# Two attentions in one kernel: sliced token loads, a later value half, a moved gate and another planner rule

## The chip, the cores and the metric

The kernel runs on one core of a Trainium2 chip. The metric is the device time of one execution in microseconds. The core has a matrix engine (TensorE, PE), whose weight loads the profile shows apart (PEld), a vector engine (VectorE, DVE), a scalar engine that makes the exponentials (ScalarE, ACT), a general engine (GpSimd, POOL), and a queue that issues most transfers (SyncE, SP). Every engine works through its own list of instructions in order.

## The reference

Two attention layers over 2048 tokens with 640 features and 32 heads of 20 stand side by side; their outputs are joined.

- A, "infini": the tokens come in four segments of 512. Within a segment, softmax attention with a causal mask; besides, a memory of all earlier segments is read with phi(q), and both are mixed by a gate g of its own for each head.
- B, "sliding block": causal attention in which a token sees the last 256 tokens.

```python
phi = lambda t: where(t > 0, t + 1.0, exp(t))
g = sigmoid(beta)
for s in range(4):                         # A, segment s
    a_dot = softmax(qs @ ks.T * scale + mask) @ vs
    a_mem = (phi(qs) @ M) / (phi(qs) @ z + 1e-6)
    o = g * a_mem + (1 - g) * a_dot
    M += phi(ks).T @ vs;  z += phi(ks).sum()
A = concat(o) @ A_wo
p = softmax(where((0 <= i - j) & (i - j < 256), q @ k.T * scale, -1e9))   # B
B = (p @ v) @ B_wo
out = concat([A, B])
```

## The kernel before, in words

The work is cut into eight chunks of 512 tokens, which alternate: A0, B0, A1, B1, A2, B2, A3, B3 (numbered 0 to 7). For each chunk there are these stages.

- Token load (`load_x`): the chunk's transposed tokens, five tiles of 128 features, into one of two buffers `xT`; 640 KB for A, 720 KB for B. Only chunk 0 is loaded as five transfers, the others as one each.
- Projections (`qk_job`, `v_job`, matmuls in `wide`, L795): q and k as five pieces of 128 columns, each five matmuls of 512 columns and a copy from PSUM by VectorE (L449); v in two halves of 16 heads, each four token tiles of five matmuls of 320 columns, with a copy (L624 for A, L629 for B). For A, v is scaled by 1-g as it is copied.
- Regroup (`regroup`): the heads are held in eight groups of four. Groups 0 to 4 lie in the projected pieces as they come. The parts of groups 5 to 7 are spread over all five pieces; once piece 4 is copied, four stores bring them to memory (L404) and four loads bring them back (L412).
- Scores (`score_batch`, L687): 20 visits a chunk, 160 in all, in a fixed order. Each fills two PSUM tiles `sc` of 1024 columns; ScalarE makes an exponential of each (L703) into a tile `pt` from a ring of 12. Masks are laid on `pt` by GpSimd (L738) or, for the window's ends, by VectorE (L720).
- Value products (`av`, L752, and `av_tile`, L773): `pt` times values, with the sum of weights as a 21st column. VectorE transposes the result (`turn`, L808) into a tile `tt`, takes the reciprocal (`norm`, L834), and GpSimd multiplies it into the output `o` (L844).
- For A: phi of k and q (`phi`; exponential L469, VectorE L484 and L490). phi(k) goes to memory (L543), comes back transposed (L538), and `dm_job` adds to the memory `mz` (L592); GpSimd writes it, with a block mask `bm` and a gate factor `ez`, into the bf16 operand `MZ4` (L598, L601). `mem` multiplies phi(q) with it; `norm` adds an epsilon to the denominator (L828), and the product `u` is added to `o` (L857).
- Output (`final`, `final_job`): `o` goes to memory (L875), comes back transposed (L894) as `oT`, and each of its four token tiles is multiplied with `wo`, 2 x 5 matmuls of 320 columns. As long as scores remain, this goes through the two banks `m` and VectorE copies (L950); after the last scores it goes through `sc`, and ScalarE or VectorE copies (L933, L937), whichever the planner has as free. An output tile `ot` (ring of 4) is stored by L1015. The last token tile of chunk 7 goes another way (`last_job`).

No instruction order is written out by hand. While the program is built, a planner (`Flow`) keeps a clock for each engine and for the transfers, with a cost for each operation (`on_pe`, `on_act`, `on_dve`, `on_pool`, `on_dma`). The loop in `body` takes, at each step, the next score visit if its operands are due, then the first waiting value product, then the next step of the first job whose need is met. A value product is put off, while TensorE is in full-width mode, if a score visit is due within 1500 ns. Queued loads are issued when they are due or when the transfers' backlog is under 2500 ns (`load_time`). Rings of buffers (`piece`, `ring`) are counted in the same clock. So a changed cost or limit can move instructions anywhere.

Of the kernel before, what the change touches and what calls it, by code (L numbers as in the profile page):

```python
# [8 lines left out]
ACT = mybir.ActivationFunctionType  # L9
# [14 lines left out]
GW = G * DH  # L24
EPS = 1e-6
NPT = 12
NTT = 5
QPOOL = 750.0
GAP = 48
NM = 20  # L30
MEM2 = [(1, 6), (0, 5), (1, 7), (0, 6)]
R2 = 120
NE = 3
NOT = 4
NSC = 3

# [21 lines left out]
class Flow:  # L58
# [3 lines left out]
    def __init__(self):  # L62
        self.pe = self.act = self.dve = self.pool = 0.0
        self.mode = None
        self.sp = self.fabric = 0.0
        self.landed = []
        self.bank_free = [0.0, 0.0]
        self.open = False
        self.left = 0
        self.later = []  # L70
        self.idle_dve = []
        self.idle_low = []
        self.blocked = []
        self.loads = []
        self.seq = 0
        self.load = {}
        self.slow = {}

    def full_rate(self, t):

# [5 lines left out]
                    self.slow[m] = had < (0.355 if self.slow.get(m - 1, True) else 0.31)  # L86
        return not self.slow[k]

    def on_pe(self, mode, ns, cols, ready=0.0):
        if mode != self.mode:  # L90
            self.pe += 97.0
            self.mode = mode
        self.pe = max(self.pe, ready)
        k = int(self.pe // STRETCH)
        self.load[k] = self.load.get(k, 0.0) + cols / 2.4
        if not self.full_rate(self.pe):
            ns += cols / 2.4
        self.pe += ns
        return self.pe + 215.0
# [40 lines left out]
    def load_time(self):  # L140

        if not self.loads:
            return None
        t = max(self.sp - 100.0, self.fabric - 2500.0)
        gate, _, due = self.loads[0]
        if gate:
            if gate() is None:
                return None
            return min(max(t, gate() - 400.0), gate() + due)
        return min(t, due)  # L150
# [34 lines left out]
class _K:  # L185
# [67 lines left out]
    def load_x(self, n):  # L253

        kind, c = self.chunks[n]
        x0 = SH if kind == "A" else 0
        src = (self.xin[kind][:, c * L:(c + 1) * L] if kind == "A" else
               self.xin[kind][c]).rearrange("(kt p) s -> p kt s", p=P)
        t = self.xs[n] = self.big.tile([P, self.KT, XC], BF16, name="xT", bufs=2)

        def main():
            if n == 0:
                for kt in range(self.KT):
                    self.nc.sync.dma_start(out=t[:, kt, x0:XC], in_=src[:, kt, :])
                    self.mark(self.f.on_dma(1, 450.0, 0.0, 400.0), n, "x", kt)
                self.mark(self.done[(n, "x", self.KT - 1)], n, "x")
                return
            self.nc.sync.dma_start(out=t[:, :, x0:XC], in_=src)
            tl = self.f.on_dma(1, 2220.0 if kind == "A" else 2440.0, 0.0, 530.0)
            self.mark(tl, n, "x")  # L270
            self.mark(tl, n, "xt")
        self.loads.insert(0, (None, main, max(12000.0, self.f.pe + 6000.0)))

    def consts_mem(self):

        nc, cp = self.nc, self.cp

        def select(t, pattern, base, mul):
            nc.gpsimd.affine_select(out=t, in_=t, pattern=pattern, compare_op=ALU.is_ge,
                                    fill=0.0, base=base, channel_multiplier=mul)
        own = cp.tile([P, 4], F32, name="own")
        nc.gpsimd.memset(own[:], 1.0)
        select(own[:], [[-HD, 4]], 0, 1)
        select(own[:], [[HD, 4]], DH - 1, -1)
        self.bm = bm = cp.tile([P, self.KT + 4, 4], F32, name="bm")
        self.ez = cp.tile([P, self.KT + 4, 4], F32, name="ez")
        nc.gpsimd.tensor_copy(out=bm[:, 0:self.KT, :],  # L290
                              in_=own[:].unsqueeze(1).to_broadcast([P, self.KT, 4]))
        sel = bm[:, self.KT:, :]
        nc.gpsimd.memset(sel, 1.0)
        select(sel, [[-2 * DH, 4], [-DH, 4]], 2 * DH, 1)
        select(sel, [[2 * DH, 4], [DH, 4]], -DH - 1, -1)
        self.eps = cp.tile([P, G], F32, name="eps")

    def consts_e(self):

        nc, e = self.nc, self.e32  # L300
        for x0, x1, g in [(0, self.KT, 0)] + [(self.KT + x, self.KT + x + 1, g)
                                              for x, (_, g) in enumerate(MEM2)]:
            n = x1 - x0
            h = e[:, 4 * g:4 * g + 4 * n].rearrange("p (x j) -> p x j", j=4)
            nc.gpsimd.tensor_tensor(out=self.ez[:, x0:x1, :], in0=self.bm[:, x0:x1, :], in1=h,
                                    op=ALU.mult)
        for j in range(4):
            rows = slice(HD * j, HD * j + HD)
            nc.gpsimd.tensor_single_scalar(
                out=self.eps[rows, :], in_=e[rows, :].rearrange(  # L310
                    "p (g j) -> p g j", j=4)[:, :, j], scalar=EPS, op=ALU.mult)

    def consts_mz(self):
        nc, cp = self.nc, self.cp
# [30 lines left out]
    def load_beta(self, beta):  # L345
# [3 lines left out]
        e = self.cp.tile([P, H], F32, name="e32")  # L349
        self.nc.scalar.activation(out=e[:], in_=b[:], func=ACT.Exp, scale=-1.0)  # L350
        self.e32 = e

    def consts_beta(self):
        nc, cp, e = self.nc, self.cp, self.e32
# [105 lines left out]
    def phi(self, in_, t, m, use):  # L460
# [13 lines left out]
        def one(in_, e, es, m, ta):  # L474
            box = []

            def s1():
                r = out(m)
                if r is None:
                    r, slot = self.piece("r", 2, 1)  # L480
                    box.append(slot)
                    r = r[:]
                box.append(r)
# [68 lines left out]
    def dm_job(self, seg, pkT, v):  # L552
# [12 lines left out]
        for some in (own, [(lambda kt, h=h: spare[:, kt, R2 * h:R2 * h + R2], R2,  # L565
# [23 lines left out]
            else:  # L589
# [5 lines left out]
        t = f.dve + 138.0  # L595
        yield self.known(2 * seg, "avs")
        blk, mz = self.blk, self.mz
        nc.gpsimd.tensor_tensor(out=blk[:, :, :, DH], in0=mz[:, :, :, DH], in1=self.ez[:],  # L598
                                op=ALU.mult)
        f.on_pool(150.0, t)  # L600
        nc.gpsimd.tensor_tensor(out=blk[:, :, :, 0:DH], in0=mz[:, :, :, 0:DH],  # L601
                                in1=self.bm[:].unsqueeze(3)
                                .to_broadcast([P, KT + 4, 4, DH]), op=ALU.mult)
        self.mark(f.on_pool(1700.0), "dm", seg)

# [71 lines left out]
    def score_batch(self, n, ent, kof, q, masks):  # L677
# [13 lines left out]
                                 skip_group_check=ref[0] in "lu")  # L691
            cols += nq
        if ent[0][1][0] in "lu":
            t = f.on_pe("row64", 40.0 * len(ent), cols / 2)
        else:
            t = f.on_pe("row", cols / 2.4 + 10.0 * len(ent), cols)
        lo = min(e[4] for e in ent)
        hi = max(e[4] + e[3] for e in ent)
        pts = []
# [43 lines left out]
    def av(self, parts, g, vof):  # L743
# [4 lines left out]
        for n_, (ref, q0, nq, c0, pts) in enumerate(parts):  # L748
# [6 lines left out]
                                 start=(n_ == 0), stop=(n_ == len(parts) - 1),  # L755
                                 tile_position=(0, HD * j), skip_group_check=True)
            cols += nq
        f.on_pe("col", cols / 2.4 + 6.0 * len(parts), cols)
        return O, bi

    def av_tile(self, parts, qt, g0, vof):
# [3 lines left out]
        for gi in range(4):  # L765
            own = sorted((p[:5] for p in parts[g0 + gi] if p[1] // P == qt),
                         key=lambda e: -e[2])
            for n_, (ref, q0, nq, c0, pts) in enumerate(own):
                v = vof(ref)
                o0 = gi * P + q0 - qt * P  # L770
                for j in range(4):
# [3 lines left out]
                                     rhs=pts[j // 2][:, j % 2, c0:c0 + nq],  # L775
                                     start=(n_ == 0), stop=(n_ == len(own) - 1),
                                     tile_position=(0, HD * j), skip_group_check=True)
                f.on_pe("col", nq / 2.4 + 6.0, nq)
        return O, bi

    def mem(self, g):
# [31 lines left out]
    def norm(self, turned, dst, add_to, last, g=None):  # L813
# [11 lines left out]

        def s1():
            if add_to:
                nc.vector.tensor_tensor(out=rr[:], in0=tv[:, :, DH],  # L828
                                        in1=self.eps[:, g:g + 1].to_broadcast([P, NB]),
                                        op=ALU.add)  # L830
                f.on_dve(100.0, t0)
                nc.vector.reciprocal(out=rr[:], in_=rr[:])
            else:
# [4 lines left out]
        def s2(t1):  # L838
            to, uslot = dst, None
            if add_to:  # L840
                while self.ring("u", 3) is None:
                    self.adds[0]()
                to, uslot = self.piece("u", 3, 1, BF16, (P, NB, DH))
            nc.gpsimd.tensor_tensor(out=to[:] if add_to else to, in0=a, in1=b, op=ALU.mult)  # L844
            t2 = f.on_pool(QPOOL, max(t1, uslot["free"]) if add_to else t1)
            self.done_with(slot, t2)
# [250 lines left out]
    def seed(self, n):  # L1097
# [13 lines left out]
        else:  # L1111
# [2 lines left out]
                  ("k", self.wA["k"], self.kA, self.phi_k(n, self.scr["pk"][c], self.pkT)  # L1114
                   if c < NSEG - 1 else None)]
            v = [self.wv_A, self.vA, True, [tx, avs, self.known("dm", c - 1)]]
        for half, pieces in enumerate(((0, 1, 2), (3, 4))):
            for what, w, dst, phi in qk:
                need = [tx, gate] + ([self.known("wB" + what, 0)] if n == 1 else [])
                add(self.qk_job(n, what, pieces, w, dst, need, self.scr[what + kind][c], phi))  # L1120
            if n == 1:
                v[3] = v[3] + [self.known("wBv", half)]
            add(self.v_job(n, half, *v))

    def body(self, xA, A_wq, A_wk, A_wv, A_wo, A_beta, xB, B_wqkv, B_wo, out2d):
# [45 lines left out]
        self.consts_mem()  # L1171
        f.on_pool(8000.0)
        f.on_dve(3000.0)
        self.load_x(1)
        self.loads[:] = self.loads[1:] + self.loads[:1]
        self.wB = {}
        pieces = lambda w: w.rearrange("p (m k c) -> p m k c", m=KT, k=KT)
        self.wB["k"] = self.load_qk("wBk", pieces(B_wqkv[1]), 0, KT, None, 17000.0)
# [27 lines left out]
        for m in range(KT):  # L1206
            first("k", m, self.kA, pk0)
            first("q", m, self.qA, None)
            if m in (1, 3):
                half = m // 2  # L1210
                add(self.job(self.v_job(0, half, self.wv_A, self.vA, True,
                                        [self.known(0, "x"), self.known("wv_A", half)])))

        bs = self.batches(chunks)
        free_after = {}
# [15 lines left out]
        while True:  # L1231
# [3 lines left out]
            if i < len(bs):  # L1235
                n, ent, ms, complete = bs[i]
                kind, c = chunks[n]
                if self.ring("pt", NPT) is not None:
# [2 lines left out]
                        for w in "kq":  # L1241
                            need.append(self.done.get((n, w, e[0])))
                    if None not in need:
                        t = max(need)
                        if t <= f.pe:
                            if n != started:
                                started = n
# [18 lines left out]
            if pend:  # L1266
# [10 lines left out]
                    need = [self.done.get(("dm", c - 1)),  # L1277
                            self.done.get((n, "pq", g) if g < KT else (n, "pq2"))]
                if None not in need and not (f.open and 0 < f.left <= 3):
                    t = max(need + [min(f.bank_free)])  # L1280
                    wait = (f.mode == "full" and soon is not None and len(pend) < 3
                            and soon < f.pe + 1500.0 and self.more(f.pe))
                    if t <= f.pe and not wait:
                        pend.pop(0)
                        self.one_group(n, kind, c, g, what, parts, left, o_t, groups_done,
# [196 lines left out]
```

## Time and profile before

| | us |
|---|---|
| median of 3 runs | 351.1 (349.35 to 351.61) |
| the profiled execution | 350.9, span 349.2 |
| busy: TensorE / ScalarE / GpSimd / VectorE | 327.0 / 312.0 / 280.3 / 269.1 |
| first exponential of scores starts | 10.44 |
| last exponential of scores ends | 334.14 |
| mean granted TensorE clock | 0.99 of full speed |

Times in the profile count from the start of the span. A line of the timeline merges instructions of one kind in a row; L-numbers are lines of the kernel before. A busy TensorE includes the latency of its pipeline, so matmuls that follow each other are better read from start to start.

### The profile page before, as it was taken

The page shows a single profiled execution, that of the slowest core. Times are in us where ns is not written, and L with a number is a line of the kernel's source. Part 1 is how long each engine was busy: PE and PEld are TensorE (multiplying, and loading weights), DVE is VectorE, ACT ScalarE, POOL GpSimd, SP SyncE. Part 2 cuts the span into 40 slices and gives each one's busy share as a digit, 9 for nine tenths or more (in the row PEclk, how much of TensorE's full clock was granted, in tenths as well). Part 3 has the DMA queues.
Part 4 walks back from the last instruction along what each step waited for, and adds up shares of the span by engine and source line. Part 5 has one row for each costly group of instructions (what it writes and reads, how often), then busy time and mean ns, then how long its engine had stood idle before and what let it go on. Part 6 is the DMA issues. An engine that isn't in the chain of part 4 may idle for free.

```text
span 349.2 us, 13489 instructions
## 1 busy us (share of the span) xinstructions
PE 327.0 (94%) x5593; PEld 167.4 (48%) x5593; DVE 269.1 (77%) x564; ACT 312.0 (89%) x345; POOL 280.3 (80%) x584
## 2 busy tenths in 40 slices
PE   6999999998999999999979999989999999999895
PEld 1433445454544345455633435545553435666573
DVE  5667568988967999998836898997867998976552
ACT  1898399999899999999969999999999999999731
POOL 2399379997788989995857989999978889799640
PEclk9999999999999999999989999999999999999899
DMA  7944736565695433057683316112543028466642
GB/s 227 344 185 84 191 67 186 135 137 128 156 210 115 81 82 116 2 116 134 176 206 77 78 30 166 27 35 46 100 113 78 2 40 206 117 154 134 156 131 98
DMA packets 70186, 42.49 MB, mean 122 GB/s; under 512 B 47437, under 2 KB 68077, under 8 KB 70125
## 3 DMA queue, kind: packets, MB, share of 16 engines
q1 hardware_dynamic: 68829, 40.65, 47.3%
q10 hardware_dynamic: 1296, 0.99, 0.9%
q8 instruction: 43, 0.70, 0.9%
q14 instruction: 18, 0.15, 0.1%
HBM read 17.62 MB, written 16.96 MB: 99 GB/s over the span
## 4 chain that ended last, share of the span: by engine, by line
PE 32%; DVE 14%; ACT 13%; POOL 8%; issue 4%; DMA 2%; ACTq 0%; SPq 0%; DVEq 0%
PE m L795 17%; ACT pt L703 13%; PE sc L687 7%; POOL pt L738 5%; PE m L752 4%; DVE tt L808 3%; PE sc L795 2%; DVE pt L720 2%; POOL o L844 1%; DMA out_dram<-ot 1%; DVE ot L950 1%; PE m L773 1%; DVE kA L449 1%; DVE vU L657 1%; DVE pq L490 1%
## 5 line engine op out<-in xcount | busy, mean ns | idle before, releaser
L703 ACT ACTIVATE pt<-sc 128x1024 bf16<-128x1024 f32 (+1 forms) x320 | 295.8, 1099 | 20.8 <-PE sc L687 18.3
L738 POOL TENSOR_SCALAR_AFFINE_SELECT pt<-pt 128x256 bf16<-128x256 bf16 x448 | 200.2, 472 | 49.6 <-ACT pt L703 42.1
L808 DVE STREAM_TRANSPOSE tt<-m 128x512 f32<-128x512 f32 x88 | 60.6, 707 | 18.6 <-PE m L752 12.3
L844 POOL TENSOR_TENSOR o<-tt,rr 128x320 bf16<-128x320 f32 x64 | 48.4, 758 | 6.2 <-DVE rr L834 6.0
L795 PEld LDWEIGHTS <-xT 128*128 128x128 bf16 x350 | 31.3, 97 | 22.1 <-issue 10.3
L687 PE MATMUL sc<-qB,kB 20*64 20x64 bf16 (+2 forms) x1728 | 39.8, 218 | 2.1 <-issue 1.4
L687 PE MATMUL sc<-qA,kA 20*128 20x128 bf16 (+3 forms) x512 | 37.4, 302 | 1.1 <-ACT pt L703 0.5
L950 DVE CAST ot<-m 128x320 bf16<-128x320 f32 x52 | 24.9, 484 | 14.3 <-PE m L795 11.4
L687 PEld LDWEIGHTS <-kB 20*64 20x64 bf16 (+1 forms) x1728 | 22.3, 99 | 27.3 <-issue 25.5
L795 PEld LDWEIGHTS <-oT 128*128 128x128 bf16 x280 | 25.1, 99 | 15.5 <-issue 4.8
L795 PE MATMUL m<-xT,wk_A 128*128 128x512 bf16 x100 | 26.3, 380 | 3.1 <-DMA wk_A<-in_A_wk_dram 1.5
L795 PE MATMUL m<-wv_A,xT 128*128 128x320 bf16 x160 | 27.0, 300 | 1.8 <-DVE vA L624 0.8
L795 PE MATMUL m<-xT,wq_A 128*128 128x512 bf16 x100 | 26.5, 381 | 0.3 <-DVE mz L592 0.3
L795 PE MATMUL m<-xT,wBq 128*128 128x512 bf16 x100 | 25.8, 380 | 0.8 <-DVE tt L808 0.5
L795 PE MATMUL m<-xT,wBk 128*128 128x512 bf16 x100 | 26.4, 389 | 0.1
L795 PE MATMUL m<-wBv,xT 128*128 128x320 bf16 x160 | 26.0, 300 | 0.3 <-DVE tt L808 0.2
L687 PEld LDWEIGHTS <-kA 20*128 20x128 bf16 x512 | 11.3, 92 | 30.0 <-issue 29.0
L720 DVE TENSOR_TENSOR pt<-pt,ends 128x1024 bf16<-128x1024 bf16 x32 | 24.9, 790 | 0.0
L795 PE MATMUL m<-wo_A,oT 128*128 128x320 bf16 x130 | 22.8, 307 | 0.7 <-DVE vA L624 0.5
L752 PE MATMUL m<-pt,vA 128*32 128x256 bf16 (+3 forms) x512 | 23.3, 302 | 0.2 <-DVE qA L449 0.2
L795 PE MATMUL m<-wo_B,oT 128*128 128x320 bf16 x120 | 21.0, 306 | 0.5 <-DVE ot L950 0.5
L449 DVE CAST qB<-m 128x512 bf16<-128x512 f32 x20 | 13.7, 687 | 7.5 <-PE m L795 7.5
(104 smaller groups left out, 410.7 us busy)
## 6 DMA issues: line engine op xcount, KB each, us to landing
scr_o<-o SPq DMA_DIRECT2D x28, 160.0 KB
out_dram<-ot SPq DMA_DIRECT2D x28, 160.0 KB
xT<-in_B_x_dram SPq DMA_DIRECT2D x4, 720.0 KB
scr_pk<-e SPq DMA_DIRECT2D x15, 128.0 KB
xT<-in_A_x_dram SPq DMA_DIRECT2D x3, 640.0 KB
scr_kA<-kA SPq DMA_DIRECT2D x16, 60.0 KB
scr_qA<-qA SPq DMA_DIRECT2D x16, 60.0 KB
kA<-scr_kA SPq DMA_DIRECT2D x16, 60.0 KB
```

The source lines that it names most:

```text
L449: nc.vector.tensor_copy(out=dst[:, m, at:at + L], in_=ps[:, :])
L490: nc.vector.tensor_tensor(out=r if len(box) == 1 else e, in0=r, in1=e, op=ALU.min)
L657: self.nc.vector.tensor_copy(out=out, in_=in_)
L687: nc.tensor.matmul(ps[j // 2][h0:h1, j % 2, c0:c0 + nq], lhsT=k[rows, g, kc + h0:kc + h1], rhs=q[rows, g, q0:q0 + nq], start=True, stop=Tr ...
L703: nc.scalar.activation(out=pt[:, :, lo:hi], in_=ps[i][:, :, lo:hi], func=ACT.Exp, scale=self.scale)
L720: nc.vector.tensor_tensor(out=blk, in0=blk, in1=self.ends[:].unsqueeze(1).to_broadcast([P, 1024 // SH, SH]), op=ALU.mult)
L738: nc.gpsimd.affine_select(out=blk, in_=blk, pattern=pat, compare_op=ALU.is_ge, fill=self.zero, base=base, channel_multiplier=mul)
L752: nc.tensor.matmul(O[HD * j:HD * j + HD, q0:q0 + nq], lhsT=v[:, VS * h:VS * h + HD], rhs=pts[j // 2][:, j % 2, c0:c0 + nq], start=(n_ == 0 ...
L795: self.nc.tensor.matmul(ps[:, 0:n], lhsT=lhsT, rhs=rhs, start=start, stop=stop)
L808: self.nc.vector.transpose(out=tt[:], in_=O[:, :])
L844: nc.gpsimd.tensor_tensor(out=to[:] if add_to else to, in0=a, in1=b, op=ALU.mult)
L950: nc.vector.tensor_copy(out=ot[:, 320 * hf:320 * hf + 320], in_=ps[:, 0:320])
```

## The change

- Token loads: every chunk's load is five transfers, queued one by one with due times 1500 ns apart. The allowed backlog of the transfers falls from 2500 to 800 ns (`BACK`).
- Chunk 0's second value half is no longer put behind piece 3; it is queued by `late_v` once the first k and q pieces of chunk 1 are queued (`AT = 0`). Chunk 1's q and k jobs come piece by piece, k and q in turn.
- Gate: `ez` is now made of exp(beta) (`g32`) and multiplies the memory's numerators (MZ4's columns 0 to 19), the plain mask its denominators; the epsilon becomes a constant, the tile `eps` and its operations go.
- Planner: `room` holds back value products and half-width score visits while more than 160 matmul instructions would have been issued within 3000 ns; a value product is put off if a visit is due within 2200 ns.
- Rings: `tt` and `rr` 5 to 4 (`NTT`), `e` 3 to 2 (`NE`), `u` 3 to 2, `r` 2 to 1.
- The copies out of PSUM keep their engines and rules.

```diff
+AT = 0
+FETCH = 160
+FETCH_NS = 3000
+BACK = 800.0
-NTT = 5
+NTT = 4
-NE = 3
+NE = 2
...
+    def room(self, n):
+        while self.issued and self.issued[0][0] <= self.pe - FETCH_NS:
+            self.issued.pop(0)
+        have = n + sum(k for _, k in self.issued)
+        t = self.pe
+        for t0, k in self.issued:
+            if have <= FETCH:
+                break
+            have -= k
+            t = t0 + FETCH_NS
+        return t
...
-        t = max(self.sp - 100.0, self.fabric - 2500.0)
+        t = max(self.sp - 100.0, self.fabric - BACK)
...
+        def part(kt):
+            self.nc.sync.dma_start(out=t[:, kt, x0:XC], in_=src[:, kt, :])
...
-            self.nc.sync.dma_start(out=t[:, :, x0:XC], in_=src)
...
+        self.loads[0:0] = [(None, lambda kt=kt: part(kt), due + 1500.0 * kt)
+                           for kt in range(self.KT)]
...
-        nc.gpsimd.tensor_tensor(out=blk[:, :, :, DH], in0=mz[:, :, :, DH], in1=self.ez[:],
+        nc.gpsimd.tensor_tensor(out=blk[:, :, :, DH], in0=mz[:, :, :, DH], in1=self.bm[:],
...
-                                in1=self.bm[:].unsqueeze(3)
+                                in1=self.ez[:].unsqueeze(3)
...
-                nc.vector.tensor_tensor(out=rr[:], in0=tv[:, :, DH],
-                                        in1=self.eps[:, g:g + 1].to_broadcast([P, NB]),
-                                        op=ALU.add)
+                nc.vector.tensor_single_scalar(out=rr[:], in_=tv[:, :, DH], scalar=EPS,
+                                               op=ALU.add)
...
+            for some in ([(m,) for m in pieces] if first else [pieces]):
+                for what, w, dst, phi in qk:
...
+                if first and some[0] == AT:
+                    add(self.late_v())
...
-            if m in (1, 3):
-                half = m // 2
-                add(self.job(self.v_job(0, half, ...)))
+            if m == 1:
+                add(self.job(v(0)))
+        self.late_v = lambda: v(1)
...
-                        t = max(need)
+                        t = max(need + [f.room(4 * len(ent)) if ent[0][1][0] in "lu" else 0.0])
...
-                    t = max(need + [min(f.bank_free)])
+                    t = max(need + [min(f.bank_free), f.room(
+                        4 * len(ps_)) if what != "mem" else 0.0])
                     wait = (f.mode == "full" and soon is not None and len(pend) < 3
-                            and soon < f.pe + 1500.0 and self.more(f.pe))
+                            and soon < f.pe + 2200.0 and self.more(f.pe))
```

## The prediction

> **What bounds the kernel now.** I read the page's first part, then ScalarE's timeline from end to end, then the other engines' timelines where ScalarE is idle, then the tail. Columns of a timeline line: start, length, engine, source line, operation, count, and in brackets the idle time before it with what ended it.
>
> ```profile
> PE 327.0 (94%) x5593; PEld 167.4 (48%) x5593; DVE 269.1 (77%) x564; ACT 312.0 (89%) x345; POOL 280.3 (80%) x584
> ```
>
> ScalarE makes 320 exponentials (two for each of 160 score visits). They run back to back over long stretches: 72 of them take 66.56 us, 0.924 each, so a visit costs ScalarE 1.85 us. First start 10.44, last end 334.14. TensorE's 94% also counts pipeline latency, but it is a close second: between visits it usually has 1.4 to 2.0 us of work. So the span is 10.4 of filling, then ScalarE's work plus the moments when it gets no scores, then a tail of 15.1 without exponentials. Those moments are short but for two:
>
> ```profile
> 32.34 3.77 ACT L703 ACTIVATE pt<-sc 128x1024 bf16<-128x1024 f32 x4
> 41.58 1.94 ACT L703 ACTIVATE pt<-sc 128x1024 bf16<-128x1024 f32 x2 [5.46 <-PE sc L687]
> ...
> 180.98 1.94 ACT L703 ACTIVATE pt<-sc 128x1024 bf16<-128x1024 f32 x2 [3.04 <-PE sc L687]
> ```
>
> The first is at visit 12 (counted from 0). Visit 12 needs head groups of q and k that go to memory and back after the fifth projection piece:
>
> ```profile
> 29.18 0.69 DVE L449 CAST kA<-m 128x512 bf16<-128x512 f32 x1 [0.46 <-PE m L795]
> 30.70 0.69 DVE L449 CAST qA<-m 128x512 bf16<-128x512 f32 x1 [0.82 <-PE m L795]
> ```
>
> ```profile
> 29.90 1.67 SPq L404 DMA_DIRECT2D scr_kA<-kA  x4
> 31.67 1.96 SPq L404 DMA_DIRECT2D scr_qA<-qA  x4
> 33.73 0.41 SPq L268 DMA_DIRECT2D xT<-in_A_x_dram  x1
> 34.25 1.92 SPq L412 DMA_DIRECT2D kA<-scr_kA  x4
> 36.73 2.67 SPq L412 DMA_DIRECT2D qA<-scr_qA  x4
> ```
>
> Last load issued at 39.40, exponentials 2.2 us later. The second is at visit 81: a copy of an output tile waits until the tile buffer's previous store has landed, and TensorE's PSUM bank with it.
>
> ```profile
> 170.79 0.40 SPq L268 DMA_DIRECT2D xT<-in_A_x_dram  x1
> 172.88 0.96 SPq L1015 DMA_DIRECT2D out_dram<-ot  x2
> ```
>
> ```profile
> 177.81 0.89 DVE L950 CAST ot<-m 128x320 bf16<-128x320 f32 x2 [2.65 <-DMA out_dram<-ot]
> ```
>
> The store was issued behind a whole token load of 640 KB. In the tail TensorE is the bound: 320-column output products, (2.74-0.30)/18 = 0.136 us each.
>
> ```profile
> 342.81 2.74 PE L795 MATMUL sc<-wo_B,xT 128*128 128x320 bf16 x19
> ```
>
> ```profile
> 345.59 0.69 ACT L933 CAST ot<-sc 128x640 bf16<-128x640 f32 x1 [2.15 <-PE sc L795]
> ```
>
> **The change, part by part.** The kernel's own planner lays the order out, so all edits move instructions. Against before, TensorE's order is the same through visit 5; it differs in visits 6 to 56; from 57 to 153 it has the same kinds in the same places; it differs again in the tail.
>
> *Later second values of chunk 0.* The 20 products of the second value half (20 x 0.136 = 2.7 us) leave the place ahead of k and q piece 4 and come after the first B pieces. Working in after's order: value products end 22.6 as before; k piece 4 (5 x 0.216 = 1.1) ends 23.7, its copy (0.69) about 24.6; q piece 4, with a visit between, ends 25.1. Its copy stands on VectorE behind a memset (1.20), a reciprocal and three small operations, so it ends about 27.6. On SP the four stores of k go at 24.8, the token keys of pieces 2 and 3 stand among the other stores, the stores of q end about 29.4, k's loads take 1.9 after the landing of its stores, and q's go from about 31.4 (stores landed, as 2 us after issue now) to 33.2. With the same 2.2 us behind the last issue, visit 12 has its scores for ScalarE at 35.4 to 36.4. ScalarE itself is ready at 35.3 to 35.9 (23.18 at visit 6, six visits, one e of 0.63, at most 0.6 of waiting at visit 9 for a PSUM bank). I take 36.3 in place of 41.58: -5.2. TensorE agrees: from visit 11 to 12 it had 21 x 0.216 + 7 x 0.136 + 0.66 + 0.33 = 6.5 us of work, now 4 x 0.216 + 0.66 + 0.33 = 1.9. Bounds: -6.3 (visit 12 at ScalarE's own pace) and -2 (q's loads 3 us later). If the lead is there, next late are the value products of groups 4 to 7, which the score-tile ring of 12 (six visits) covers.
>
> *The second block, visits 12 to 40.* What TensorE no longer does early it does here: summed with the trace's median time from start to start of each kind of product, it has 52.7 us here, 49.5 before. Before, the stretch took 57.4 us (scores of visit 12 at 40.7, of visit 41 at 98.1), with 1.7 us of small ScalarE waits in it.
>
> ```profile
> 57.00:74.00 17.00, 16.66 (x349) 8.84 (x346) 15.68 (x30) 16.98 (x21) 16.86 (x34) 1.00 0.63 164
> 74.00:98.10 24.10, 22.14 (x476) 12.07 (x475) 20.40 (x44) 22.93 (x29) 19.61 (x46) 1.00 0.60 154
> ```
>
> (Busy PE, PEld, DVE, ACT, POOL.) ScalarE, TensorE and GpSimd are all near full in the first row. The phi exponentials (1.06 and 0.65) also move from visits 25 to 35 to visits 29 to 40, where after puts its heavier TensorE stretches (2.1 to 2.5 us), so they hide each other. I take -0.3; bounds -1.7 and +3.2.
>
> *Token loads in slices.* Seven loads become 35 DMAs: 28 more issues of about 0.42 us, 12 us of SP's queue, and each DMA also waits for the one eight before it. Where they stand matters: the chunk-2 load now goes behind q's and k's loads instead of ahead (part of the -5.2), and at visit 80 two output stores go ahead of four of the five slices. The tile buffers there are now four different ones, and the first reused was stored several microseconds earlier with 128 KB instead of 640 KB in front of it. So the 2.65 us wait goes; the stretch has 2.6 us of TensorE work for 1.85 of ScalarE, so not all 3.04 comes back: -2.4 (bounds -3.0 and -1.0). At the start the slices stand before the B weights; those are first used at 25.1 and 27.6, and the DMA engines run dry at about 22.3 now (share 0.09 from 22 to 24), so 3 us of delay are covered; past that each microsecond costs one.
>
> [...] In this trace, slices of 128 KB with others in flight moved 317 to 337 GB/s from 6 to 10 us. [...]
>
> *Gate in the numerators.* Four GpSimd operations (0.9 us) go, one exponential of 128x32 (0.23) comes where ScalarE waits for 4.65 us, 24 additions of 0.365 become scalar additions (nearest rows 0.17 and 0.37). VectorE is 77% busy and behind others: 0, at best -0.5.
>
> *Smaller rings.* Transposed tiles 5 to 4, e 3 to 2, u 3 to 2, r 2 to 1. Counting in the trace from each transpose back to the GpSimd product four tiles earlier, the closest are 0.61, 0.62, 0.63 and 0.80 us (303.6, 287.4, 209.9, 227.0 us); for u two back, 2.78. So 0 while GpSimd is no later than now; without that cover, see below.
>
> *Tail.* After the last visit TensorE now has 90 of the 320-column products, before 65: three output tiles fewer are done in the middle. Five come before the last value products instead of 20, so 25 x 0.136 = +3.4, all after the last token tile (53 instead of 19). Bounds +2.7 (better clock) and +4.5 (the transposed load of chunk 6 now issues behind a store and another load and lands about a microsecond ahead of need).
>
> Sum: -5.2 - 0.3 - 2.4 + 3.4 = -4.5 on a span of 349.2, so 344.7. The profiled execution took 350.9, 1.7 more than its span, and the median of the runs is 351.1. Forecast 346.5.
>
> **The rivals.**
>
> *The second block takes it back.* If TensorE or GpSimd sets the pace from 36 to 98 us, the 3.2 us come on top instead of -0.3: 350.0. For it: GpSimd busy 16.86 of 17.00. Against: ScalarE's own need there (29 visits x 1.85, less 0.43 for each of eight short ones, plus 5.1 of phi: 55.4) is still more than TensorE's 52.7. 17%.
>
> *Everything helps.* Visit 12 at -6.3, second block -1.7, visit 81 -3.0, tail +3.0: 349.2 - 8.0 + 1.7 = 342.9. 13%.
>
> *It doesn't do what it says.* SP is in order; if the token-key stores between the k and q stores wait for VectorE, q's loads go as late as now and -5.2 becomes about -0.7: 351.0. 7%.
>
> *Slower: the ring of four.* A transpose that finds its buffer still in use blocks VectorE, with it the PSUM bank and TensorE. The blocker is a product standing on GpSimd behind up to four selects, 4 x 0.445 = 1.8 us. It decides once GpSimd runs 0.7 us later than now, at 4 places; at 2.6 us later at 7 (next margins 2.46, 2.59, 2.59). 4 to 7 x 1.8 = 7 to 13, so 353.7 to 359; I take 356. For it: GpSimd is saturated in the B chunks. Against: the margins are positive everywhere now. 18%.
>
> **How the numbers follow.** The forecast holds 45%, between 345 and 349. One per cent, 3.5 us, is about what a measurement of this kernel can tell from no change; the border is 347.6. Faster: 13 + three quarters of 45 = 47%; same: the rest of it, 17 and 7, 35%; slower 18%. The range reaches from the best case to the lower part of the slow one: 342.5 to 354.5.
>
> **What would show it.** Right: visit 12's exponentials at 35.5 to 37; no VectorE wait on an output store near visit 80 and under 1 us of ScalarE wait at visit 81; visit 40 five to six microseconds earlier; 18 to 19 us from the last exponential to the end. Wrong: transposes that wait for GpSimd products, visit 12 after 38, visit 40 less than 3 us ahead, or a tail that waits for a transposed load.

## The result and the profile after

The changed kernel took 345.7 us in the median of 4 runs (344.84 to 347.2), the kernel before 351.2: ratio 0.9859, 95% interval 0.9811 to 0.9908. Measured again with the experiments it took 346.4 beside 350.2, ratio 0.9926 (0.9893 to 0.9960). Ratios leave out disturbed runs, so they need not be those of the medians. So the gain was 1.4% in the first measurement and 0.7% in the second. The profiled execution took 345.8, span 344.1, against 350.9 and 349.2.

The page's first part; ScalarE is now busy for 91% of the span:

```profile
PE 319.8 (93%) x5555; PEld 165.6 (48%) x5593; DVE 266.8 (78%) x560; ACT 312.7 (91%) x347; POOL 278.5 (81%) x580
```

ScalarE's timeline of the changed kernel, the lines around the two waits that the prediction was about, and then the waits of about 1 us:

```profile
30.34 36.18 ACT L727 ACTIVATE pt<-sc 128x1024 bf16<-128x1024 f32 x40 [1.05 <-PE sc L711]
...
159.28 59.03 ACT L727 ACTIVATE pt<-sc 128x1024 bf16<-128x1024 f32 x64
...
243.46 57.19 ACT L727 ACTIVATE pt<-sc 128x1024 bf16<-128x1024 f32 x62 [1.08 <-PE sc L711]
301.51 7.55 ACT L727 ACTIVATE pt<-sc 128x1024 bf16<-128x1024 f32 x8 [0.86 <-POOL pt L762]
...
315.79 9.62 ACT L727 ACTIVATE pt<-sc 128x1024 bf16<-128x1024 f32 x10 [0.96 <-PE sc L711]
```

The 40 exponentials that run on from 30.34 hold visit 12, which starts at 35.99; the 5.46 us are gone. The 64 from 159.28 hold visit 81; the 3.04 us are gone. Idle time of ScalarE between the first and the last exponential fell from 16.2 to 7.7 us. Three waits of about 1 us are new; the prediction had none of them.

The granted clock of TensorE differs too. This row of the page gives it for 40 slices of the span (9 is full), for the kernel before and then for the changed one:

```profile
PEclk9999999999999999999989999999999999999899
PEclk9999999999999999999999999999999999999999
```

In the trace of before TensorE had half its clock from 178.45 to 181.86 us and from 328.63 to 332.05, around the waits of visit 81 and of visits 158 and 159; in that of the changed kernel it never had. By an estimate from these two lengths, half of 2 x 3.41, that is worth up to 3.4 us. In the second measurement the 12 runs of the changed kernel all had a mean clock of 0.998 or more, of the 29 runs of before 7 had, and their median is 348.3. At full clock the gain is then 1.9 us, half of what the medians show. The first stretch begins as TensorE comes out of a pause of 1.87 us, which the change removes; but pauses of 1.31 and 1.46 us in other traces below are followed by no such stretch, and whether the change itself keeps the clock up was not isolated.

VectorE's, SP's and TensorE's timelines, the steps that lead to visit 12:

```profile
23.75 0.69 DVE L473 CAST kA<-m 128x512 bf16<-128x512 f32 x1 [0.32 <-PE m L819]
...
27.27 0.68 DVE L473 CAST qA<-m 128x512 bf16<-128x512 f32 x1
```

```profile
24.47 1.57 SPq L428 DMA_DIRECT2D scr_kA<-kA  x4
...
27.97 1.56 SPq L428 DMA_DIRECT2D scr_qA<-qA  x4
...
30.09 1.67 SPq L436 DMA_DIRECT2D kA<-scr_kA  x4
31.87 1.42 SPq L436 DMA_DIRECT2D qA<-scr_qA  x4
...
33.84 2.82 SPq L289 DMA_DIRECT2D xT<-in_A_x_dram  x5
```

```profile
35.53 0.49 PE L711 MATMUL sc<-qA,kA 20*128 20x256 bf16 x8
```

The last load of q is issued by 33.29. TensorE makes visit 12's scores at 35.53 without having waited, and ScalarE takes them at 35.99, straight behind visit 11. So the loads no longer set visit 12: ScalarE's own pace does. The tail, on TensorE and ScalarE:

```profile
333.27 3.29 PE L819 MATMUL sc<-wo_A,oT 128*128 128x320 bf16 x23
336.39 4.24 PE L819 MATMUL sc<-wo_B,xT 128*128 128x320 bf16 x30
```

```profile
340.67 0.69 ACT L956 CAST ot<-sc 128x640 bf16<-128x640 f32 x1 [2.02 <-PE sc L819]
```

From the last exponential's end (325.41) to the end of the span there are 18.7 us, before 15.1.

### The profile page after: what moved, and what is told of

It is laid out like the page before. It is cut to its first block, busy times and chain, and to the rows that moved or that the text cites. A ratio compares the mean times of both kernels' runs of the same rounds, so it can differ in the third digit from the quotient of the medians.

```text
span 344.1 us, 13492 instructions
## 1 busy us (share of the span) xinstructions
PE 319.8 (93%) x5555; PEld 165.6 (48%) x5593; DVE 266.8 (78%) x560; ACT 312.7 (91%) x347; POOL 278.5 (81%) x580
## 3 DMA queue, kind: packets, MB, share of 16 engines
q10 hardware_dynamic: 1440, 1.16, 1.1%
## 4 chain that ended last, share of the span: by engine, by line
PE 51%; DVE 20%; ACT 15%; issue 6%; POOL 5%; DMA 2%; DVEq 0%; ACTq 0%
PE m L819 29%; ACT pt L727 14%; PE sc L711 10%; PE m L776 6%; DVE tt L832 4%; PE sc L819 4%; POOL pt L762 3%; DMA wk_A<-in_A_wk_dram 2%; PE m L797 2%; DVE pt L744 2%; DVE kA L473 2%; DVE qB L473 1%; DVE vU L681 1%; DVE ot L973 1%; DVE qA L473 1%
## 5 line engine op out<-in xcount | busy, mean ns | idle before, releaser
L819 PEld LDWEIGHTS <-xT 128*128 128x128 bf16 x350 | 31.4, 97 | 21.5 <-issue 9.6
L711 PE MATMUL sc<-qB,kB 20*64 20x64 bf16 (+2 forms) x1728 | 39.0, 217 | 2.0 <-issue 1.1
L711 PE MATMUL sc<-qA,kA 20*128 20x128 bf16 (+3 forms) x512 | 35.9, 300 | 1.1 <-ACT pt L727 0.5
L973 DVE CAST ot<-m 128x320 bf16<-128x320 f32 x46 | 22.2, 485 | 9.3 <-PE m L819 9.1
L819 PE MATMUL m<-xT,wBq 128*128 128x512 bf16 x92 | 25.8, 380 | 3.6 <-DVE qA L473 1.4
L819 PE MATMUL m<-xT,wk_A 128*128 128x512 bf16 x91 | 25.8, 393 | 2.4 <-DMA wk_A<-in_A_wk_dram 0.9
L819 PE MATMUL m<-xT,wq_A 128*128 128x512 bf16 x89 | 24.8, 383 | 1.2 <-issue 0.3
L819 PE MATMUL m<-xT,wBk 128*128 128x512 bf16 x90 | 24.9, 381 | 0.9 <-DVE qB L473 0.2
L711 PEld LDWEIGHTS <-kA 20*128 20x128 bf16 x512 | 10.6, 91 | 28.8 <-issue 28.3
L744 DVE TENSOR_TENSOR pt<-pt,ends 128x1024 bf16<-128x1024 bf16 x32 | 23.0, 732 | 0.0
L819 PE MATMUL m<-wo_A,oT 128*128 128x320 bf16 x120 | 20.4, 300 | 0.3 <-DVE ot L973 0.3
L819 PE MATMUL m<-wo_B,oT 128*128 128x320 bf16 x110 | 18.8, 300 | 0.3 <-DVE ot L973 0.2
```

What stands on the lines that cost most here:

```text
L711: nc.tensor.matmul(ps[j // 2][h0:h1, j % 2, c0:c0 + nq], lhsT=k[rows, g, kc + h0:kc + h1], rhs=q[rows, g, q0:q0 + nq], start=True, stop=Tr ...
L744: nc.vector.tensor_tensor(out=blk, in0=blk, in1=self.ends[:].unsqueeze(1).to_broadcast([P, 1024 // SH, SH]), op=ALU.mult)
L819: self.nc.tensor.matmul(ps[:, 0:n], lhsT=lhsT, rhs=rhs, start=start, stop=stop)
L973: nc.vector.tensor_copy(out=ot[:, 320 * hf:320 * hf + 320], in_=ps[:, 0:320])
```

## The experiments

All kernels below ran in three groups, each beside the kernel before (medians 349.3, 350.2 and 350.4). The first exponential starts anywhere from 9.1 to 11.1 us, as the first weights land, so the times of this table are counted from it. Line numbers in a kernel's profile are its own. "Visit 12" is the start of its exponentials; "last" is the end of the last exponential; "left" are the 320-column products after the last scores (the 65 and 90 of the prediction leave out ten products of the last token tile).

| kernel | median us | ratio (95%) | visit 12 | last | tail | left |
|---|---|---|---|---|---|---|
| before | 351.2 | 1 | 31.1 | 323.7 | 15.1 | 75 |
| changed, again | 346.4 | 0.9926 (0.9893-0.9960) | 25.7 | 315.0 | 19.2 | 100 |
| late_alone | 346.0 | 0.9917 (0.9885-0.9949) | 25.8 | 314.6 | 19.8 | 100 |
| late_and_slices | 346.3 | 0.9929 (0.9895-0.9962) | 26.5 | 316.1 | 19.1 | 100 |
| no_slices | 347.0 | 0.9939 (0.9906-0.9971) | 25.7 | 315.8 | 19.3 | 100 |
| no_late | 347.5 | 0.9957 (0.9929-0.9985) | 29.3 | 318.2 | 17.0 | 85 |
| slices_alone | 349.5 | 1.0026 (0.9988-1.0065) | 29.7 | 319.1 | 18.1 | 93 |
| shift | 347.7 | 0.9967 (0.9929-1.0006) | 25.7 | 317.2 | 19.2 | 100 |
| fetch144 | 344.6 | 0.9867 (0.9821-0.9913) | 25.7 | 315.2 | 17.2 | 91 |
| fetch144, again | 344.5 | 0.9870 (0.9821-0.9919) | 26.2 | 316.5 | 17.0 | 91 |
| fetch140 | 346.7 | 0.9924 (0.9887-0.9962) | 26.1 | 320.4 | 16.0 | 56 |
| fetch128 | 351.6 | 1.0072 (1.0037-1.0107) | 26.6 | 326.7 | 14.7 | 31 |
| late_fetch144 | 345.5 | 0.9900 (0.9859-0.9940) | 25.7 | 316.1 | 17.3 | 91 |

### Which edit brings the gain

Whole token loads again (no_slices):

```diff
-        self.loads[0:0] = [(None, lambda kt=kt: part(kt), due + 1500.0 * kt) for kt in range(self.KT)]
+        self.nc.sync.dma_start(out=t[:, :, x0:XC], in_=src)   # queued as one load
```

> The changed kernel with the token loads of chunks 1 to 7 as one DMA each again; its TensorE order is that of the changed kernel, visit for visit. Theory: the slices alone took away the wait at visit 81, because the output stores no longer stand behind 640 KB of tokens. Then a VectorE copy of an output tile near visit 80 waits 2 to 3 us for a store again, visit 81 comes 2.4 to 3.4 us later, visit 12 stays at 36, and the time is 348.1 to 349.1 us. Rival: the wait went because the other edits moved the earlier output tiles in time. Then the copy waits under 0.5 us and the time is within 1 us of 345.7.

The copy waited 1.37 us and ScalarE 0.46 at visit 81: neither the 2 to 3 us of the theory nor quite the rival's nothing.

The second value half back at its place, and with it chunk 1's q and k pieces in threes and twos again (no_late); "late half" stands for both below:

```diff
-            if m == 1:
-                add(self.job(v(0)))
+            if m in (1, 3):
+                add(self.job(v(m // 2)))
```

> The changed kernel with the second value half of chunk 0 back behind piece 3 and the first B chunk's pieces in threes and twos again; slices, rings and gate stay. Theory: visit 12 goes back to 41 to 42 us (5.5 later), visit 81 keeps its gain, and 85 instead of 100 of the 320-column products stand after the last scores (15 x 0.136 = 2.0 us less at the end): 345.7 + 5.5 - 2.0 = 349.2 us. Rival: the later value half only moves the wait, since TensorE has the same products to make by visit 40; then visit 40 comes within 2 us of the changed kernel's 89.9 and the time is 345 to 347.

Visit 12 waits again, but only 3.66 us, and visit 81 keeps its gain. Counted from the first exponential, visit 40 came 5.8 us after the changed kernel's, so the lead is not made up on the way, as the rival had it; the tail is 1.7 us shorter than the changed kernel's 18.7. The theory was 1.7 us too high: from visit 80 to 116 this kernel is 5.0 us behind the changed one, near the 5.5 of the theory, but it gets about 3 back at visits 117, 148 and 155, where the changed kernel has its three new waits and this one has none.

Only these two edits (late_and_slices), with the others undone:

```diff
-NTT = 4
+NTT = 5
-NE = 2
+NE = 3
-BACK = 800.0
+BACK = 2500.0
 ...      # u and r rings 3 and 2, gate factor in the denominators, no limit, 1500 ns
```

> Only the later second value half and the sliced token loads; rings of 5, 3, 3 and 2, the gate in the denominators, the old load threshold and waiting rule. Theory: the other edits are worth nothing, so the time is within 1 us of 345.7, with visit 12 at 36 and visit 81 without its wait. Rival: the smaller rings cost GpSimd or VectorE something that the margins of 0.7 us do not show, or the gate saves VectorE time; then the time differs by 1.5 us or more, with the difference in the chunks of kind A after the first.

With no_slices' edit on top of it, the late half stands alone (late_alone).

> The kernel before with the later second value half of chunk 0 alone. Theory of separate terms: visit 12 at 36, visit 81 still waits about 3 us, 100 products of 320 columns after the last scores; 3 us more than the changed kernel, 348.1 to 349.1 us. Rival: the gains are not separate, because an earlier chunk 0 also moves the output tiles around visit 80 away from the token load; then visit 81 waits under 1 us and the time is 345 to 347.

The first bears out its theory: beside these two edits, rings, gate and load threshold are worth nothing that can be measured. The second bears out its rival. This is SP's, then VectorE's, then ScalarE's timeline of late_alone, with a whole token load at 165.58:

```profile
165.58 0.40 SPq L291 DMA_DIRECT2D xT<-in_A_x_dram  x1
166.08 2.32 SPq L566 DMA_DIRECT2D scr_pk<-e  x1
168.52 0.36 SPq L1038 DMA_DIRECT2D out_dram<-ot  x1
```

```profile
171.77 0.49 DVE L973 CAST ot<-m 128x320 bf16<-128x320 f32 x1 [0.92 <-DMA out_dram<-ot]
```

```profile
160.08 20.50 ACT L726 ACTIVATE pt<-sc 128x1024 bf16<-128x1024 f32 x22
```

The store still stands behind the load, but the copy waits 0.92 instead of 2.65 us, and 22 exponentials run through visit 81 without a break: a copy's wait of 0.92 us costs ScalarE nothing here, where 1.37 in no_slices cost it 0.46. The fourth cell of the table of two edits is late_and_slices with no_late's edit (slices_alone):

> The kernel before with the sliced token loads alone, which closes the table of two edits (both 346.3, late half alone 346.0, all but the late half 347.5, each beside a kernel before of 349.3). Theory: the two edits overlap. The slices let the loads of q and k go ahead of chunk 2's tokens and take away the wait at visit 81 by themselves, so counted from the first exponential visit 12 comes 1 to 2 us earlier than before and visit 81 waits under 1 us: 1.5 to 3 us faster than the kernel before. Rival: what the kernel without the late half gained came from the smaller rings and the gate; then visit 12 and visit 81 stay as before and the time is within 1 us of the kernel before.

In its trace visit 12 came 1.4 us earlier and visit 81 did not wait, as the theory said:

```profile
39.36 1.94 ACT L731 ACTIVATE pt<-sc 128x1024 bf16<-128x1024 f32 x2 [4.03 <-PE sc L715]
...
169.16 11.23 ACT L731 ACTIVATE pt<-sc 128x1024 bf16<-128x1024 f32 x12 [0.30 <-PE sc L715]
```

But 93 products are left and the tail is 3.1 us longer, and the runs show no gain (1.0026), against the theory's 1.5 to 3 us. At a mean clock of 0.998 or more it is even slower: 349.5 us (11 of 12 runs) beside 347.6 for before (11 of 29); the late half alone has 346.0 (all 12) beside 348.3 (13 of 35). So the late half carries the change, and it takes both waits away: with it the slices add nothing that the ratios tell apart (0.9917 without, 0.9929 with). Without it, no_late, which has rings, gate, threshold and waiting rule besides the slices, is faster than the slices alone (0.9957, interval up to 0.9985, against 1.0026, from 0.9988); its tail is 1.1 us shorter, and which of these edits does it was not isolated.

### The three new stops

At each of the three new ScalarE waits TensorE stops in the middle of a row of like products, for nothing that the profile shows. TensorE's timeline of the changed kernel, three places:

```profile
243.24 0.22 PE L711 MATMUL sc<-qB,kB 20*64 20x64 bf16 x3 [0.86 <-issue]
...
300.44 0.21 PE L797 MATMUL m<-pt,vU 128*32 128x64 bf16 x3 [0.92 <-issue]
...
314.86 0.19 PE L797 MATMUL m<-pt,vL 128*32 128x64 bf16 x1 [1.13 <-issue]
```

The page's table of queues has the instruction queue that suits them: 43 transfers, 0.70 MB, so 16 KB each.

```profile
q8 instruction: 43, 0.70, 0.8%
```

In the trace the transfers before the three stops end at 241.86, 298.98 and 313.46, so TensorE goes on 1.38, 1.46 and 1.40 us after them. Records are the PE and PEld rows of the trace, counted in order; the trace of the changed kernel lacks 38 matmul records (5555 of 5593 in the page's first line). The changed kernel ran once more without any edit:

> The changed kernel once more, unaltered, to have its time beside the others of this call and a second trace of it. Theory on the three moments of 0.86 to 1.13 us in which TensorE stops without a releaser (242.4, 299.5 and 313.7 us; TensorE records 7584, 9371 and 10139): they belong to the program, so they return at the same records within 5. Rival: they are chance, and come elsewhere or not at all. Time 345 to 347 us.

The stops came back at records 9371 (0.95 us) and 10139 (1.18); the one at 7584 fell below 0.45. Three of the kernels above with the same TensorE order in the later chunks (no_slices, late_alone, late_and_slices) have them at 9370 or 9371 and 10138 or 10139 too.

Then the warm-up products in `warm_up` were split (shift):

```diff
+            if k < 3:
                 self.wide(ps, z[:, 0:P], z[:, 0:L], L, True, True)
+            else:                          # 8 products of 48 columns, 3 times
+                ...
```

> The changed kernel with three of the six warm-up products of 512 columns replaced by eight products of 48 columns each, so that every later TensorE instruction stands 42 places further on in the program; order, tiles and waits are unchanged. Theory: TensorE's program arrives in blocks of 16 KB (the 43 transfers of the instruction queue), 256 instructions each, and the stalls are waits for a block. Then the stalls of visits 117, 148 and 155 go or change size by more than 0.4 us, others come elsewhere, each of them ends 1.3 to 1.5 us after the end of a 16 KB transfer, at a record whose number modulo 256 is again near 155 to 160. Rival: they come from the work at those visits (a bank, a tile, GpSimd) and stay at visits 117, 148 and 155 with 0.8 to 1.1 us each. Time by the theory 343 to 350 us, as the blocks fall; by the rival 345 to 347.

TensorE's timeline of shift:

```profile
301.73 0.21 PE L805 MATMUL m<-pt,vL 128*32 128x64 bf16 x4 [1.17 <-issue]
...
324.72 1.25 PE L827 MATMUL m<-wo_B,oT 128*128 128x320 bf16 x8 [1.46 <-issue]
330.37 0.21 PE L805 MATMUL m<-pt,vL 128*32 128x64 bf16 x3 [0.55 <-issue]
```

With the stop that ends at 316.44 (1.31 us) these are records 9370, 10138, 10650 and 10906: the numbers of the kernels without the shift, though each number is now an instruction 42 places earlier in the work, and all four leave 154 on division by 256. Each ends 1.3 to 1.5 us after a 16 KB transfer; the instruction queue has 44 of them here, one more than in every other kernel. Visit 117's stop went and one came before visit 159 (ScalarE waits 1.19). Visits 148 and 155 kept theirs, against what I had written: 42 instructions are a third of a visit's 128, so a stop can move and stay in the same visit. The record numbers decide for the blocks. Missing records explain why the remainder is not always the same: 155 with 38 missing at the end (the changed kernel), 154 with 39 (shift, late_alone, no_slices), 193 with none (the stop of before, at record 10689), and 155 + 38 = 154 + 39 = 193.

In the changed kernel's trace a transfer ends 2.3 us in the median after TensorE's first record of a block, and at its three stops TensorE goes on 1.4 us after a transfer's end: by an estimate from the two about 3.7 us from a block's first record until TensorE can go on. At the three stops it was 3.8, 4.3 and 5.4 us, and the 256 records before had passed in 2.8, 3.2 and 4.1; the rest is the stop. A score visit of 64 products with 64 weight loads passes in about 0.7 us (0.71 at 297.96 us), so by an estimate from these times such visits and their value products go through a block faster than others. That TensorE asks for a block only when it begins the one ahead of it is the author's estimate from the same times and was not isolated. The price is measured: 0.86 to 1.13 us a stop.

### Products in the tail or ahead of it

`room` limits the products in 3 us to 160 and the waiting rule was widened to 2200 ns; taking either away changes no instruction of the program. Lower limits do move them:

```diff
-FETCH = 160
+FETCH = 144        # and 140, 128
```

> The changed kernel with the planner's limit of products in 3 us at 144 instead of 160. At 160 the limit changes not one instruction; at 144 eleven visits from 37 on get other work between them, and 91 instead of 100 products of 320 columns stand after the last scores. Theory: the limit keeps TensorE from running ahead of its program, so one or more of the three stalls of about 1 us go and the tail is 9 x 0.136 = 1.2 us shorter: 343 to 345 us. Rival: the products only move from the tail into visits that then wait for their scores; within 1 us of the changed kernel.

> The changed kernel with the same limit at 128: 31 instead of 100 products of 320 columns are left after the last scores, 69 x 0.136 = 9.4 us of TensorE work that moves ahead of it. Theory: TensorE's idle time between the first and the last exponential (17.9 us in the changed kernel) can take part of these products, and the stalls go; the tail becomes about 9 us shorter and the last exponential comes 4 to 8 us later: 341 to 345 us. Rival: ScalarE waits for scores as long as the products take, the last exponential comes 9 us later or more, and the time is 346 to 352.

> The changed kernel with the planner's limit at 140: 56 instead of 100 products of 320 columns after the last scores, other visits changed in 15 places, nearly all from 152 on. It stands between the limit of 144 (91 products, 1.8 us faster than the changed kernel) and of 128 (31 products, 5.3 us slower). Theory: products put ahead of the last scores cost ScalarE their own length, 44 x 0.136 = 6.0 us, and what the tail saves is no more than that; the last exponential comes about 5 us later, the tail is about 5 us shorter than 18.7, and the time is within 1.5 us of the changed kernel's 346.4. Rival: the last visits have room for the products, as at 144, and the time falls below 343.

At 144 the last exponential ends where it did (315.2 against 315.0 from the first) and the tail is 2.1 us shorter. The nine products are 1.2 of it; a stop of 0.70 us that the other trace has in its tail, and this one has not, is most of the rest. As the theory had it, stops go: none at records 9371 and 10139, one of 0.42 us at 7584 and a new one of 1.31 us at 9883, again 155 modulo 256. But the last exponential is no earlier for it. At 128 the rival holds: the last exponential comes 11.7 us later and the tail gives back 4.6. ScalarE's timeline shows the last of the places where it waits:

```profile
332.84 2.86 ACT L727 ACTIVATE pt<-sc 128x1024 bf16<-128x1024 f32 x3 [1.70 <-PE sc L711]
...
341.42 0.48 ACT L1009 CAST pkT<-sc 128x384 bf16<-128x384 f32 x1 [3.44 <-DVE pq L1007]
```

Visits wait for scores behind 15 or 16 output products in a row, 2.3 to 2.4 us of TensorE's time, and in the tail ScalarE now waits 3.4 us for the last token tile's own chain. In this trace TensorE also had half its clock in the tail, from 340.29 to 347.12 us, and none of the 12 runs had a clock of 0.998 or more; so the 14.7 us of this tail are no floor. At 140 it is in between: the last exponential 5.4 later, the tail 3.2 shorter where I had expected 5 (here too half the clock, from 338.35 to 341.76), and the time is that of the changed kernel.

> The changed kernel with the limit at 144 once more, unaltered, as the version that has been the fastest. Theory: a tail about 2 us shorter at the same time of the last exponential, so 344 to 345.5 us again. Rival: the 1.8 us came from the spread of the runs (the changed kernel has run from 344.4 to 347.9); then it is within 0.7 us of 346.4.

The late half alone with that limit:

> The kernel before with two edits alone: the later second value half of chunk 0, and the planner's limit of products in 3 us at 144. Theory: the late half carries the gain of the change, and the limit shortens the tail by the same products as in the changed kernel, so the time is that of the changed kernel with the limit at 144, 344.0 to 345.5 us beside a kernel before of about 350. Rival: the limit helped there only by the way the program's blocks fell on the dense visits; here they fall otherwise, and the time is that of the late half alone, 346 to 347.

The limit at 144 stands the repeat: all its 12 runs lie between 343.3 and 345.2, the changed kernel's 16 between 344.8 and 347.9. It is the fastest version here. With the late half alone it gives 345.5, at the upper edge of its theory; against 346.0 for the late half alone that is not settled.

## Why the prediction was right, and where not

Forecast 346.5, span 344.7; the first measurement gave 345.7 and the trace 344.1. Term by term, from the exponentials' starts in the two traces:

| stretch | predicted | measured |
|---|---|---|
| to visit 12 | -5.2 | -5.6 |
| visits 12 to 44 | -0.3 | -0.3 |
| visits 44 to 80 | 0 | +0.2 |
| visits 81 to 84 | -2.4 | -3.5 |
| three stops (117, 148, 155) | none | +3.0 |
| visits 156 to 159 | none | -2.7 |
| after the last exponential | +3.4 | +3.6 |
| sum (0.1 in the other stretches) | -4.5 | -5.1 |

*Chunk 0's second half.* Right in its steps: k's stores were forecast for 24.8 and went at 24.47, q's copy was to end at 27.6 and ended at 27.95, q's loads were to go from 31.4 to 33.2 and went from 31.87 to 33.29; visit 12 was to start at 36.3 and started at 35.99. What set it was not q's loads, which the 36.3 was built on, but ScalarE, forecast to be ready at 35.3 to 35.9; it waited 1.05 us at visit 9, where at most 0.6 had been allowed for. So visit 12 came at ScalarE's own pace, the lower bound of this term, 0.7 us later than that bound had it; the two chains end so close together that the number alone does not tell them apart.

*The second block.* Right at visit 44, 5.9 us ahead. At visit 40 the lead was 7.2 us, not five to six: the exponentials of phi stand elsewhere, and a wait of 0.78 at visit 44 gave that back. The rows that made the rival are as full as before,

```profile
57.00:74.00 17.00, 16.43 (x386) 9.28 (x392) 15.16 (x32) 16.91 (x21) 16.74 (x38) 1.00 0.62 154
```

ScalarE at 16.91 of 17.00 with TensorE and GpSimd just under it, so ScalarE set the pace, as its larger need had said.

*Visit 81.* The wait went, but the term was mis-sized by 1.1 us. The 2.6 us of TensorE work that were to hold ScalarE up were too many: from visit 80's scores to visit 81's the changed kernel took 1.99 us without a wait (169.86 to 171.85). In the trace of before this stretch says little about the work, since TensorE had half its clock there. The same sixteen products, before and after:

```profile
178.49 0.87 PE L752 MATMUL m<-pt,vB 128*32 128x256 bf16 x16
```

```profile
170.81 0.50 PE L776 MATMUL m<-pt,vB 128*32 128x256 bf16 x16
```

From the first value product behind the copy to the visit's scores there were 1.90 us before (178.35 to 180.25) and 1.16 after (170.69 to 171.85). The reason given for the lost wait was one of two that each suffice: late_alone shows the wait gone with whole loads. How the earlier order shortens the copy's wait to 0.92 was not isolated.

*Stops.* The 3.0 us of the three stops had no term. The trace of before had one such stop too, in the middle of visit 158's scores, and nothing was made of it.

*The end.* The tail was right in its sum. One reading in it was not: 15 products, not five, come before the last value products; the 25 more in all hold. They had left visits 35 to 39, and the changed kernel stays that far behind from there on. The -2.7 us of visits 156 to 159 are no effect of these products: between the scores of these visits both kernels make 10, 2 and 9. Before, the stop and the half clock stood there:

```profile
328.74 0.29 PE L687 MATMUL sc<-qB,kB 20*128 20x128 bf16 x3 [1.41 <-issue]
...
331.47 0.61 PE L687 MATMUL sc<-qB,kB 20*128 20x128 bf16 x16
```

A like row of the changed kernel, at full clock:

```profile
320.80 0.40 PE L711 MATMUL sc<-qB,kB 20*128 20x128 bf16 x16
```

So the step that failed is the pricing of TensorE by its products alone, with stops and the granted clock put at nothing. What that left out, +3.0 of stops in the changed kernel, -2.7 of a stop and half clock in the trace of before and -1.1 at visit 81, nearly cancels. That the sum came within 0.6 us of the span is in part luck.

*Rings, gate.* Nothing, as forecast. Counted as in the prediction, the closest transpose of the changed kernel starts 0.68 us after its buffer came free (295.6 us), so the slower rival had as little room as the prediction had counted, and did not come about. The 317 to 337 GB/s that the prediction gives to slices of 128 KB were moved by larger loads: in the trace of before the last of the five slices had landed by 6.16 us, and no packet of theirs (1024 B) is among those from 6 to 10 us.

## What to carry to other kernels

When two edits may each remove a wait, price the wait once and ask what each leaves if the other stands. Before pricing a stretch from a trace, look at the granted clock in it: a time read at half clock is not the time of the work (the sixteen products above: 0.87 us at half, 0.50 at full). On an engine with many short instructions, count instructions as well as time: here 256 of them in 2.8 to 4.1 us were followed by stops of about 1 us.

## What the runs showed of the hardware

In the trace of before the instruction queue made 43 transfers of 16 KB beside TensorE's 11186 products and weight loads, and in shift the stops stood at records 9370, 10138, 10650 and 10906, multiples of 256 apart: blocks of 256 instructions, a weight load counting as one. A transfer took 1.0 us in the median of the changed kernel's trace (up to 1.8), and TensorE went on 1.38 to 1.46 us after its end at that kernel's three stops. Where the stops came they stood at fixed record numbers from run to run and through other edits, while their length varied (at records 9370 and 9371 0.45 us in late_and_slices, 0.95 in after_again, 1.17 in shift). TensorE's clock was granted in full or in half (1.0 and 0.5 in the trace of before); in the three traces that have halves ahead of the last 2 us of the span (before, fetch140, fetch128) they last 3.41 us, once twice that. The first exponential started between 9.1 and 10.4 us in kernels that begin alike: a wait of TensorE for the first weights (0.67 us in the changed kernel's trace, none in no_late's) comes and goes. That is as much as most of the edits here are worth.
